# Attention over hop tokens: residual added by VectorE out of PSUM, row variances by ScalarE squares, and a new order inside an iteration

## The chip, the cores and the metric

The kernel runs on one core of a Trainium2 chip. A core has a matrix engine (TensorE; PE in the profile, its weight loads PEld), VectorE (DVE), ScalarE (ACT), GpSimd (POOL) and a queue engine for transfers (SyncE, SP). Each engine works through its own instructions in order; they meet at semaphores. The metric is the device time of one execution in microseconds (us), the median of several runs.

## What is computed

The reference propagates the features of 10,000 nodes seven times over a graph of 160,000 edges, which gives eight tokens of 128 features for each node, and then runs one self-attention block over each node's eight tokens and a weighted readout:

```python
    tok = jnp.stack(toks, axis=1)                      # (N, K+1, D)
    t = _layernorm(tok, axis=-1)
    q   = jnp.einsum('nkd,de->nke', t, wq)
    key = jnp.einsum('nkd,de->nke', t, wk)
    v   = jnp.einsum('nkd,de->nke', t, wv)
    scale = 1.0 / (D ** 0.5)
    attn = _softmax(jnp.einsum('nkd,nld->nkl', q, key) * scale, axis=-1)
    o = jnp.einsum('nkl,nld->nkd', attn, v)
    o = tok + jnp.einsum('nkd,de->nke', o, wo)
    r = _layernorm(o, axis=-1)
    alpha = _softmax(jnp.einsum('nkd,d->nk', r, w_r), axis=-1)
    return jnp.einsum('nk,nkd->nd', alpha, o)
```

All of it is in fp32 in the attention stage.

## The kernel before

First come the hops (class `Hops`, lines 34 to 600), which leave the eight tokens in DRAM as arrays `tok[k]`. The change leaves them as they are. Then `attention` runs. It takes the rows in groups of 16 nodes: 16 nodes x 8 tokens = 128 partitions, 128 features along the free dimension, and 16 groups make a supergroup (`SG`), so there are 40 supergroups, the last one with a single group. Its instructions stand on each engine in the order in which the Python code emits them; nothing reorders them.

The algebra is folded so that the layer norm needs few passes. `M` is the centred product of wq and wk, `Wv` that of wv and wo, with two more columns that give, for each token, a readout term of the value (column 128) and one of the token itself (129). The factor 1/sqrt(variance) of each row is applied later: by rows to the scores, by columns through small products that spread a row's factor over the eight rows of its node (`same_node`, a product with a 0/1 matrix `same`).

For one supergroup i the steps are, with the engine that does them:

- `load` (SP): eight transfers, one for each token index, into the tile `x`; six buffers.
- `xT` (PE, then a copy by ACT): transposes of the 16 groups, four at a time ("quarters", q = 0 to 3).
- `uT` (PE, ACT copy): M times xT, a quarter at a time. `val` (PE, ACT copy): xT times Wv, three groups at a time, into `v`.
- `norms` (DVE): `bn_stats` of the rows of `x` of one supergroup and of the rows of `o` of an older one, then `rstd` for both together: variance, and three Newton steps for the inverse root. It gives `rs` (for the scores) and `lb` (for the readout, from `w`).
- `extras` (DVE): `rb`, the row factor and the value term laid out by token.
- `score` (PE): 64 small products of uT and xT into the PSUM tile `ps`.
- `same_node` (PE): spreads `rb` (of i) and `lb` (of i - 3) into the PSUM tile `sm`.
- `soft1` (DVE), `soft_exp` (ACT), `soft2` (DVE, POOL), `soft3` (DVE transpose, POOL copies): the softmax; the result is a block-diagonal matrix `PT`. `soft2` also gives `w`, the readout logit before its norm.
- `attend` (PE, ACT copy): for each quarter a product of the identity with `x` (the residual) and four products PT times v, summed in one PSUM tile `po`, copied to `o`.
- `read1` (DVE), `read_exp` (ACT), `read2` (DVE, POOL), `read3` (PE), `store` (DVE copy of `f`, SP transfers): the softmax over tokens and the weighted sum.

The loop interleaves the stages of several supergroups. In iteration i it does load(i+3); soft1(i-1); then quarter by quarter xT(i+1), uT(i), val(i), attend(i-2), with norms(i+1, i-3) in two halves, the rest of the softmax of i-1 at quarters 1 and 2, the readout of i-4 at quarters 2 and 3, scores in two halves at quarters 1 and 3, and at the end of quarter 3, in this order on PE, the node sums of i and i-3 and the readout product of i-4; `store(i-4)` closes the iteration. There are 45 iterations, from -1 to 43.

PSUM tiles share buffers by tag: the tiles of xT, uT and val have three between them (tag "a"), `po` has two, `ps`, `sm` and `pf` one each. A PE product into a full set of buffers waits until the reader of the oldest is done.

Of the kernel before, what the change touches and what calls it, by code (L numbers as in the profile page):

```python
# [591 lines left out]
SG = 16  # L592
# [41 lines left out]
def attention(ctx, tc, tok, out, wq, wk, wv, wo, w_r, ngrp=N // 16):  # L634
# [6 lines left out]
    xp, tp, vp, op_, wp, sp = pool("axp", 6), pool("atp", 2), pool("avp", 3), pool("aop", 4), pool("awp", 2), pool("asp", 4)  # L641
    pp = pool("app", 1, space=PSUM)


    ip = cp.tile([128, 128], I32, name="ip")
# [29 lines left out]
    w4 = cp.tile([128, 4, 128], F32, name="w4")  # L675
    for i, w in enumerate((wq, wk, wv, wo)):
        nc.sync.dma_start(w4[:, i, :], w)
# [13 lines left out]
    Wv = cp.tile([128, 130], F32, name="Wv")  # L691
# [18 lines left out]
    def rstd(st):  # L710

        d, v, y, z = (sp.tile([128, 2, SG], F32, name="r" + c) for c in "dvyz")
        V.tensor_tensor(d, st[:, :, :, 1], st[:, :, :, 4], op=ALU.subtract)
        V.scalar_tensor_tensor(d, d, 0.25, d, op0=ALU.mult, op1=ALU.mult)
        V.tensor_tensor(v, st[:, :, :, 2], st[:, :, :, 5], op=ALU.add)
        V.scalar_tensor_tensor(v, v, 1.0 / D, d, op0=ALU.mult, op1=ALU.add)
# [9 lines left out]
    sgs = [(s, min(SG, ngrp - s)) for s in range(0, ngrp, SG)]  # L726
    S = [dict() for _ in sgs]

    def load(i):
        s, n = sgs[i]  # L730
        x = S[i]["x"] = xp.tile([128, SG, 128], F32, name="x")
        for k in range(8):
            src = bass.AP(tensor=tok[k].tensor, offset=tok[k].offset + s * 16 * 128, ap=[[n * 128, 16], [128, n], [1, 128]])
            nc.sync.dma_start(x[k::8, :n, :], src)

    quarters = lambda i, h=None: [(a, min(a + 4, sgs[i][1])) for a in (range(0, SG, 4) if h is None else (8 * h, 8 * h + 4)) if a < sgs[i][1]]
# [23 lines left out]
    def val(i, c):  # L760
        a, b = 3 * c, min(3 * c + 3, sgs[i][1])
        if c == 0:
            S[i]["v"] = vp.tile([128, SG, 130], F32, name="v")
        if a >= b:
            return
        p = pp.tile([128, 512], F32, name="pv", tag="a", bufs=3)[:, :390].rearrange("p (g d) -> p g d", d=130)
# [16 lines left out]
    def score(i, h):  # L783
        if h == 0:
            S[i]["s"] = pp.tile([128, SG, 32], F32, name="ps", tag="s", bufs=1)
        for g in range(8 * h, min(8 * h + 8, sgs[i][1])):
            for c in range(0, 128, 32):
                T.matmul(S[i]["s"][c:c + 32, g, :], S[i]["uT", h][:, g - 8 * h, c:c + 32], S[i]["xT"][:, g, c:c + 32],
                         start=True, stop=True, tile_position=(0, c))
# [15 lines left out]
    def soft1(i):  # L805
        n = sgs[i][1]
        c = wp.tile([128, SG, 4, 8], F32, name="c4")[:, :n]
        V.tensor_tensor(c, S[i]["s"][:, :n].rearrange("p g (n k) -> p g n k", k=8),
                        in4[:, None, :, None].to_broadcast([128, n, 4, 8]), op=ALU.mult)
        rk = wp.tile([128, SG, 8], F32, name="rk")[:, :n]  # L810
        V.tensor_tensor(rk, S[i]["sm"][:, 0, :n], S[i]["rs"][:, :, None].to_broadcast([128, n, 8]), op=ALU.mult)
        e = S[i]["e"] = wp.tile([128, SG, 8], F32, name="e")[:, :n]
        V.tensor_reduce(e, c.rearrange("p g n k -> p g k n"), axis=X, op=ALU.add)
        V.tensor_mul(e, e, rk)
# [4 lines left out]
    def soft_exp(i):  # L819
        A.activation(S[i]["e"], S[i]["e"], AF.Exp)  # L820

    def soft2(i):
# [11 lines left out]
        y = wp.tile([128, SG, 8], F32, name="y")[:, :n]  # L834
        V.tensor_tensor(y, e, S[i]["sm"][:, 1, :n], op=ALU.mult)
# [12 lines left out]
    def norms(i, j, h):  # L848
        if h == 0:
            st = norms.st = sp.tile([128, 2, SG, 6], F32, name="st")  # L850
            if not (ok(i) and ok(j)) or sgs[i][1] < SG:
                V.memset(st, 1.0)
        st = norms.st
        if ok(i):
            for g in range(8 * h, min(8 * h + 8, sgs[i][1])):
                V.bn_stats(st[:, 0, g, :], S[i]["x"][:, g, :])  # L856
        if ok(j):
            for g in range(8 * h, min(8 * h + 8, sgs[j][1])):
                V.bn_stats(st[:, 1, g, :], S[j]["o"][:, g, :])  # L859
        if h == 1:  # L860
            y = rstd(st)
            if ok(i):
                S[i]["rs"] = y[:, 0, :sgs[i][1]]
            if ok(j):
                n = sgs[j][1]
                l = S[j]["l"] = sp.tile([128, SG], F32, name="l")[:, :n]
                V.tensor_mul(l, S[j]["w"], y[:, 1, :n])
                r = S[j]["lb"] = wp.tile([128, SG, 8], F32, name="lb")
                V.tensor_tensor(r[:, :n], l[:, :, None].to_broadcast([128, n, 8]), id8[:, None, :].to_broadcast([128, n, 8]), op=ALU.mult)
# [36 lines left out]
    def store(i):  # L906
        s, n = sgs[i]
        f = wp.tile([128, 2, 128], F32, name="f")
        for h in range(0, n, 8):
            m = min(8, n - h)  # L910
            V.tensor_copy(f[:16 * m, h // 8, :], S[i]["f"][:16 * m, h // 8, :])
# [6 lines left out]
    load(0)  # L918
    load(1)
    for i in range(-1, n + 4):  # L920
        if ok(i + 3):
            load(i + 3)
        if ok(i - 1):
            soft1(i - 1)
        for q in range(4):
            if q == 1 and ok(i - 1):
                soft_exp(i - 1)
                soft2(i - 1)
            if q == 2 and ok(i - 4):
                read1(i - 4)  # L930
            if q == 2 and ok(i - 1):
                soft3(i - 1)
            if q == 3 and ok(i - 4):
                read_exp(i - 4)
                read2(i - 4)
            if q % 2 == 0:
                norms(i + 1, i - 3, q // 2)
            if ok(i + 1):
                xT(i + 1, q)
            if ok(i):  # L940
                uT(i, q)
                for c in ((0,), (1, 2), (3, 4), (5,))[q]:
                    val(i, c)
            if ok(i - 2):
                attend(i - 2, q)
            if q % 2 == 1 and ok(i):
                if q == 3:
                    extras(i)
                score(i, q // 2)
            if q == 3:  # L950
                sm = pp.tile([128, 4, SG * 8], F32, name="sm", tag="m", bufs=1).rearrange("p a (g k) -> p a g k", k=8)
                if ok(i):
                    S[i]["sm"] = sm
                    m = sgs[i][1]
                    same_node(sm[:, 0:2, :m], S[i]["rb"][:, :, :m])
                if ok(i - 3):
                    m = sgs[i - 3][1]
                    S[i - 3]["lc"] = sm[:, 2, :m]
                    same_node(sm[:, 2, :m], S[i - 3]["lb"][:, :m])
                if ok(i - 4):  # L960
                    read3(i - 4)
        if ok(i - 4):
            store(i - 4)


# [37 lines left out]
```

## Time and profile before

| What | us | Where from |
|---|---|---|
| Median of three runs | 4508.32 | times (4507.62 to 4515.4) |
| The profiled execution | 4508.36 | its own time |
| Its span | 4506.6 | page |
| PE busy in the span | 4015.8 (89%) | page, part 1 |
| DVE busy | 3529.0 (78%) | page, part 1 |
| ACT busy | 2521.5 (56%) | page, part 1 |
| POOL busy | 1256.0 (28%) | page, part 1 |
| First instruction of the attention stage (SP, weights) | 3670.58 | order of time of SP |
| One steady iteration | 19.90 to 19.93 | eight periods from 3872.60 on |
| PE, DVE, ACT, POOL busy in it | 19.18, 17.03, 9.84, 4.35 | mean of the eight periods |

Matmuls are pipelined and their ends are modelled, so a busy PE is not PE at its peak. A line of the order of time gives the start of a run of like instructions, how long the run lasted, engine, source line, operation, output and input tiles with their shapes, how many, and in brackets how long the engine was idle before it and who released it. DVE and ACT start the next instruction a little before the last one's recorded end; the distance from start to start is what an instruction costs its engine. An fp32 product shows as two records.

### The profile page before, as it was taken

The numbers are of one execution on the slowest core, as the hardware profiler recorded it, in microseconds if no ns is written. First come the engines' busy times: TensorE is split into PE (matmuls) and PEld (weight loads), VectorE is DVE, ScalarE is ACT, GpSimd is POOL, SyncE is SP. The second block draws the span as 40 slices with busy tenths as digits, with TensorE's granted clock in tenths as the row PEclk, the third lists the DMA queues.
The fourth block names the chain that finished last, engine by engine and source line by source line (L and its number), as shares of the span: only waits on it lengthen the run. The fifth ranks groups of instructions, "written<-read, shape, count | busy, mean of one in ns | idle before, by whom it ended". The sixth has DMA issues, their size and how long they took to land.

```text
span 4506.6 us, 170913 instructions
## 1 busy us (share of the span) xinstructions
PE 4015.8 (89%) x74352; PEld 3266.3 (72%) x74352; DVE 3529.0 (78%) x7740; ACT 2521.5 (56%) x5159; POOL 1256.0 (28%) x1423
## 2 busy tenths in 40 slices
PE   0566389999998999999999999999999989999996
PEld 0456366766766888888888888888888867777774
DVE  5888799999996777777777777777766668888887
ACT  3000036565666777777777777777766645544542
POOL 0000024334343333333333333333333322222221
PEclk9887689999998999999999999999999989999998
DMA  3000044454455555555555555555555541221210
GB/s 115 1 1 1 1 132 149 140 155 149 142 154 187 182 180 177 183 185 183 178 182 181 179 182 184 177 184 184 181 163 169 164 128 52 65 63 56 65 56 10
DMA packets 296789, 588.20 MB, mean 131 GB/s; under 512 B 46895, under 2 KB 198541, under 8 KB 290781
## 3 DMA queue, kind: packets, MB, share of 16 engines
q1 hardware_dynamic: 218893, 509.90, 34.3%
q0 software_dynamic: 17696, 36.28, 3.8%
q10 hardware_dynamic: 59440, 31.03, 2.4%
q8 instruction: 582, 9.54, 0.8%
q14 instruction: 178, 1.46, 0.1%
HBM read 447.66 MB, written 129.38 MB: 128 GB/s over the span
## 4 chain that ended last, share of the span: by engine, by line
PE 51%; DVE 32%; issue 9%; DMA 4%; POOL 2%; ACT 1%; SPq 1%; ACTq 0%; DVEq 0%; POOLq 0%
PE p L442 20%; PE acc L426 20%; PE ta L270 3%; DVE w L406 3%; DVE st L859 3%; DVE st L856 2%; DVE o L183 2%; DVE w L403 2%; DMA rb<-srow 2%; DVE ro L265 2%; PE tb L335 1%; POOL r L461 1%; DVE R L183 1%; DVE oh L177 1%; DVE ux L190 1%
## 5 line engine op out<-in xcount | busy, mean ns | idle before, releaser
L445 ACT CAST eb<-p 128x512 f16<-128x512 f32 x3634 | 1859.9, 607 | 738.9 <-PE p L442 723.6
L445 DVE CAST eb<-p 128x512 f16<-128x512 f32 x1896 | 1180.2, 683 | 461.3 <-PE p L442 460.7
L442 PE MATMUL p<-tab,w 128*32 128x256 f16 x44240 | 1426.2, 274 | 30.1 <-ACT eb L445 14.3
L426 PE MATMUL acc<-eb,w 128*128 128x256 f16 (+1 forms) x11060 | 1409.4, 274 | 3.1 <-DVE indeg L483 3.0
L442 PEld LDWEIGHTS <-w 128*32 128x32 fp8e4 x44240 | 1118.1, 96 | 268.2 <-issue 185.4
L418 POOL DMA_INDIRECT og<-tabd,oidx x553 | 620.4, 1122 | 2217.8 <-PE acc L432 1426.1
L426 PEld LDWEIGHTS <-w 128*128 128x128 fp8e4 x11060 | 1019.2, 98 | 270.5 <-issue 156.4
L461 POOL TENSOR_SCALAR r<-s,ctok 128x128 f32<-128x128 f32 x553 | 451.2, 816 | 341.4 <-DVE indeg L483 170.5
L560 DVE SCALAR_TENSOR_TENSOR tab<-s,c,tab 128x128 f16<-128x128 f32 x395 | 139.2, 352 | 182.5 <-ACT tab L559 181.1
L434 DVE TENSOR_REDUCE s<-acc 128x128 f32<-128x256 f32 x553 | 234.2, 423 | 41.2 <-PE acc L432 30.7
L406 DVE TENSOR_TENSOR w<-dsl,iof 128x2560 fp8e4<-128x2560 f16 x79 | 222.5, 2816 | 1.2 <-ACT dsl L351 1.2
L257 ACT ACTIVATE U<-U 128x160 f16<-128x160 f32 x25 | 7.6, 304 | 384.5 <-PE U L250 384.5
L768 PEld LDWEIGHTS pv<-Wv,xT 128*128 128x128 f32 x1250 | 165.1, 192 | 75.7 <-issue 57.0
L780 PEld LDWEIGHTS po<-v,pT 128*128 128x128 f32 x1250 | 164.4, 192 | 74.8 <-issue 74.8
L270 PE MATMUL ta<-o,ro 128*128 128x160 f16 x1250 | 132.0, 284 | 93.3 <-DVE ro L265 93.3
L781 ACT COPY o<-po 128x512 f32<-128x512 f32 (+1 forms) x157 | 91.8, 584 | 210.9 <-PE po L780 210.9
L270 PEld LDWEIGHTS <-ro 128*128 128x128 f16 x1250 | 127.0, 121 | 97.4 <-DVE ro L265 97.0
L559 ACT ACTIVATE tab<-s,c 128x128 f16<-128x128 f32 x395 | 158.6, 401 | 62.0 <-DVE s L434 7.4
L748 ACT COPY xT<-pt 128x512 f32<-128x512 f32 (+1 forms) x157 | 91.1, 580 | 166.0 <-PE pt L747 165.9
L768 PE MATMUL pv<-Wv,xT 128*128 128x130 f32 x1250 | 165.8, 276 | 0.0
L780 PE MATMUL po<-v,pT 128*128 128x128 f32 x1250 | 165.1, 275 | 0.0
L250 PE MATMUL U<-oh,tri 128*128 128x80 f16 x1250 | 62.2, 221 | 114.7 <-DVE oh L177 114.7
(245 smaller groups left out, 4291.4 us busy)
## 6 DMA issues: line engine op xcount, KB each, us to landing
w<-gsd SPq DMA_DIRECT2D x474, 640.0 KB
rb<-srow SPq DMA_DIRECT2D x79, 640.0 KB
gsd<-w SPq DMA_DIRECT2D x79, 640.0 KB
tok<-r SPq DMA_DIRECT2D x546, 64.0 KB
x<-tok SPq DMA_DIRECT2D x273, 128.0 KB
tabd<-tab ACTq DMA_DIRECT2D x395, 64.0 KB
og<-tabd,oidx POOLq DMA_INDIRECT x553, 4.0
x<-in_x SPq DMA_DIRECT2D x39, 128.0 KB
```

Of the source, the lines that this page charges most:

```text
L270: T.matmul(ta, ro[:, j, :, i], o12[:, j, :, i], start=j + i == 0, stop=j + i == NP)
L406: V.tensor_tensor(w[:, NJ * 128:].rearrange("p (j d) -> p j d", d=128), dsl[:, g, :, None].to_broadcast([128, NJ, 128]), self.iof1[:, None ...
L418: G.indirect_dma_start(out=og, out_offset=None, in_=tabd, in_offset=bass.IndirectOffsetOnAxis(ap=self.oidx[:, t:t + 1], axis=0))
L426: T.matmul(acc[:, :m], w[:, (NJ + J) * 128:(NJ + J + 1) * 128], e[:, j, :m], start=J == 0, stop=False)
L434: V.tensor_reduce(s, acc[:, 0:256].rearrange("p (h d) -> p d h", h=2), axis=X, op=ALU.add)
L442: T.matmul(p[32 * q:32 * q + 32, j], w[:, s * CAP:(s + 1) * CAP], tab[:, s, :], start=True, stop=True)
L445: (A.copy if evac(jj) else V.tensor_copy)(e[:, :, 0:256], p.rearrange("p j h d -> p j (h d)"))
L461: self.nc.gpsimd.tensor_scalar(r, s, ct[:, t:t + 1], None, op0=ALU.mult)
L559: A.activation(new[:, t, 0:128], s, AF.Copy, scale=c1[:, t:t + 1])
L560: V.scalar_tensor_tensor(new[:, t, 128:256], s, c1[:, t:t + 1], new[:, t, 0:128], op0=ALU.mult, op1=ALU.subtract)
L768: T.matmul(p[:, g - a, :], S[i]["xT"][:, g, :], Wv, start=True, stop=True)
L780: T.matmul(p[:, g - a, :], PT[i % 2][:, g, :], S[i]["v"][:, g, :128], start=False, stop=g == b - 1, skip_group_check=True)
```

## The change

The parts of the diff, in the order of one iteration:

- `attend` no longer multiplies the identity with `x` and no longer has ACT copy the result. A new `resid` has VectorE add `po` (PSUM) and `x` (SBUF) into `o`.
- The rows of `x` no longer go through `bn_stats`. A new `squares` has ScalarE compute (x0 - x)^2 for each group, x0 being the row's first feature, with the sum along the row as a second output (`sq`); a new column 130 of `Wv` gives, out of `val`, the row's mean of x relative to x0 up to sign, and `norms` takes its square from the mean of squares.
- `bn_stats` of `o` stand apart in `stats`; `norms(i, i-3)` runs once an iteration, at quarter 2, and calls `extras` itself.
- In `soft1a` a reduce over four becomes two adds. The readout term in column 129 is copied by ACT into a ninth column of `y` and summed by the reduce that was there already; before, an add did it.
- ACT copies `f` in `store`; before, VectorE did.
- Within an iteration `val` comes in quarters 0 and 1, `uT` in 2 and 3, and all scores at the end. The node sums `sm` of i-1 and i-4 and the readout product of i-5 follow the first quarter's transposes, an iteration later than before; there are 46 iterations, from -1 to 44.
- Supergroup 0 is loaded through ACT's queue, and the weights and this load come ahead of the set-up of constants.

```diff
+    load(0, nc.scalar)
...
-    Wv = cp.tile([128, 130], F32, name="Wv")
+    Wv = cp.tile([128, 131], F32, name="Wv")
...
+    V.tensor_scalar(Wv[:, 130:131], ident[:, 0:1], -1.0, 1.0 / D, op0=ALU.mult, op1=ALU.add)
...
-        T.matmul(p[:, :b - a], ident, S[i]["x"][:, a:b, :], start=True, stop=False, skip_group_check=True)
         for g in range(a, b):
-            T.matmul(p[:, g - a, :], PT[i % 2][:, g, :], S[i]["v"][:, g, :128], start=False, stop=g == b - 1, skip_group_check=True)
-        A.copy(S[i]["o"][:, a:b, :], p[:, :b - a])
+            T.matmul(p[:, g - a, :], PT[i % 2][:, g, :], S[i]["v"][:, g, :128], start=True, stop=True)
+        S[i]["po", q] = p
+
+    def resid(i, q):
+        a, b = 4 * q, min(4 * q + 4, sgs[i][1])
+        if a < b:
+            V.tensor_tensor(S[i]["o"][:, a:b, :], S[i]["po", q][:, :b - a], S[i]["x"][:, a:b, :], op=ALU.add)
+
+    def squares(i, q):
+
+        if q == 0:
+            S[i]["sq"] = sp.tile([128, SG], F32, name="sq")
+        for g in range(4 * q, min(4 * q + 4, sgs[i][1])):
+            j = jp.tile([128, 128], F32, name="junk")
+            A.activation(j, S[i]["x"][:, g, :], AF.Square, bias=S[i]["x"][:, g, 0:1], scale=-1.0, accum_out=S[i]["sq"][:, g:g + 1])
...
+        d = wp.tile([128, SG, 2, 8], F32, name="c2")[:, :n]
+        V.tensor_tensor(d, c[:, :, 0:2], c[:, :, 2:4], op=ALU.add)
+        e = S[i]["e"] = wp.tile([128, SG, 8], F32, name="e")[:, :n]
+        V.tensor_tensor(e, d[:, :, 0], d[:, :, 1], op=ALU.add)
...
-        V.tensor_reduce(e, c.rearrange("p g n k -> p g k n"), axis=X, op=ALU.add)
...
     def soft_exp(i):
+        n = sgs[i][1]
+        y = S[i]["y"] = wp.tile([128, SG, 9], F32, name="y")[:, :n]
+        A.copy(y[:, :, 8:9], S[i]["v"][:, :n, 129:130])
         A.activation(S[i]["e"], S[i]["e"], AF.Exp)
...
-        V.tensor_tensor(w, w, S[i]["v"][:, :n, 129], op=ALU.add)
...
+            V.tensor_mul(d, S[i]["v"][:, :n, 130], S[i]["v"][:, :n, 130])
+            V.scalar_tensor_tensor(v[:, 0, :n], S[i]["sq"][:, :n], 1.0 / D, d, op0=ALU.mult, op1=ALU.subtract)
...
-            V.tensor_copy(f[:16 * m, h // 8, :], S[i]["f"][:16 * m, h // 8, :])
+            A.copy(f[:16 * m, h // 8, :], S[i]["f"][:16 * m, h // 8, :])
```

The body of the loop after the change:

```python
    for i in range(-1, n + 5):

        if ok(i + 3):
            load(i + 3)
        if ok(i - 1):
            soft1a(i - 1)
        for q in range(4):
            if ok(i + 1):
                xT(i + 1, q)
            if q == 0:
                sm = pp.tile([128, 4, SG * 8], F32, name="sm", tag="m", bufs=1).rearrange("p a (g k) -> p a g k", k=8)
                if ok(i - 1):
                    S[i - 1]["sm"] = sm
                    m = sgs[i - 1][1]
                    same_node(sm[:, 0:2, :m], S[i - 1]["rb"][:, :, :m])
                    soft1b(i - 1)
                if ok(i - 4):
                    m = sgs[i - 4][1]
                    S[i - 4]["lc"] = sm[:, 2, :m]
                    same_node(sm[:, 2, :m], S[i - 4]["lb"][:, :m])
                if ok(i - 5):
                    read3(i - 5)
            if ok(i):
                for c in range(3 * q, 3 * q + 3) if q < 2 else ():
                    val(i, c)
                for c in range(2 * q - 4, 2 * q - 2) if q >= 2 else ():
                    uT(i, c)
            if q == 0 and ok(i - 1):
                soft_exp(i - 1)
            if q == 1 and ok(i - 4):
                read_exp(i - 4)
            if ok(i + q // 2):
                squares(i + q // 2, (q + 2) % 4)
            if q == 0 and ok(i - 5):
                store(i - 5)
            if ok(i - 2):
                attend(i - 2, q)
            if q == 3 and ok(i):
                score(i)

            if q < 2 and ok(i - 3):
                stats(i - 3, 8 * q, 8 * q + 8)
            if q == 2 and ok(i - 4):
                read2(i - 4)
            if q == 2:
                norms(i, i - 3)
            if ok(i - 2):
                resid(i - 2, q)
            if q == 0 and ok(i - 1):
                soft2(i - 1)
                soft2b(i - 1)
            if q == 0 and ok(i - 4):
                read1(i - 4)
            if q == 1 and ok(i - 1):
                soft3(i - 1)
```

More of the change, by code (lines that the diff above doesn't have):

```diff
@@ L640, in attention, with load @@
     cp = pool("acp", 1)
-    xp, tp, vp, op_, wp, sp = pool("axp", 6), pool("atp", 2), pool("avp", 3), pool("aop", 4), pool("awp", 2), pool("asp", 4)
+    xp, tp, vp, op_, wp, sp, jp = (pool(*a) for a in (("axp", 6), ("atp", 2), ("avp", 3), ("aop", 4), ("awp", 2), ("asp", 4), ("ajp", 2)))
     pp = pool("app", 1, space=PSUM)
+    sgs = [(s, min(SG, ngrp - s)) for s in range(0, ngrp, SG)]
+    S = [dict() for _ in sgs]
+    def load(i, queue=nc.sync):
+        s, n = sgs[i]
+        x = S[i]["x"] = xp.tile([128, SG, 128], F32, name="x")
+        for k in range(8):
+            src = bass.AP(tensor=tok[k].tensor, offset=tok[k].offset + s * 16 * 128, ap=[[n * 128, 16], [128, n], [1, 128]])
+            queue.dma_start(x[k::8, :n, :], src)
+    w4 = cp.tile([128, 4, 128], F32, name="w4")
+    for i, w in enumerate((wq, wk, wv, wo)):
+        nc.sync.dma_start(w4[:, i, :], w)
+    load(0, nc.scalar)
     ip = cp.tile([128, 128], I32, name="ip")
@@ L708, in attention, with rstd @@
         AB.append(a)
[L710 to L716, printed above, removed]
+    def rstd(v):
+        y, z = (sp.tile([128, 2, SG], F32, name="r" + c) for c in "yz")
         V.tensor_scalar(v, v, 1e-5, None, op0=ALU.add)
@@ L724, in rstd @@
         return y
[L726 to L736, printed above, removed]
     def xT(i, q):
@@ L845, in soft3, with stats @@
             G.tensor_copy(PT[i % 2][c:c + 32, :n, c:c + 32], t[c:c + 32, :n * 32].rearrange("p (g k) -> p g k", k=32))
[L848 to L853, printed above, removed]
+    def stats(j, a, b):
+        if a == 0:
+            S[j]["st"] = sp.tile([128, SG, 6], F32, name="st")
+        for g in range(a, min(b, sgs[j][1])):
+            V.bn_stats(S[j]["st"][:, g, :], S[j]["o"][:, g, :])
@@ L854, in norms @@
+    def norms(i, j):
+        v = sp.tile([128, 2, SG], F32, name="rv")
+        if not (ok(i) and ok(j)) or sgs[i][1] < SG:
+            V.memset(v, 1.0)
         if ok(i):
-            for g in range(8 * h, min(8 * h + 8, sgs[i][1])):
-                V.bn_stats(st[:, 0, g, :], S[i]["x"][:, g, :])
+            n = sgs[i][1]
+            d = sp.tile([128, SG], F32, name="rx")[:, :n]
+            V.tensor_mul(d, S[i]["v"][:, :n, 130], S[i]["v"][:, :n, 130])
+            V.scalar_tensor_tensor(v[:, 0, :n], S[i]["sq"][:, :n], 1.0 / D, d, op0=ALU.mult, op1=ALU.subtract)
@@ L857, in norms @@
         if ok(j):
[L858 to L869, printed above, removed]
+            n = sgs[j][1]
@@ new lines, in norms @@
+            st = S[j]["st"][:, :n]
+            d = sp.tile([128, SG], F32, name="rd")[:, :n]
+            V.tensor_tensor(d, st[:, :, 1], st[:, :, 4], op=ALU.subtract)
+            V.scalar_tensor_tensor(d, d, 0.25, d, op0=ALU.mult, op1=ALU.mult)
+            V.tensor_tensor(v[:, 1, :n], st[:, :, 2], st[:, :, 5], op=ALU.add)
+            V.scalar_tensor_tensor(v[:, 1, :n], v[:, 1, :n], 1.0 / D, d, op0=ALU.mult, op1=ALU.add)
+        y = rstd(v)
+        if ok(j):
+            n = sgs[j][1]
+            l = S[j]["l"] = sp.tile([128, SG], F32, name="l")[:, :n]
+            V.tensor_mul(l, S[j]["w"], y[:, 1, :n])
+            r = S[j]["lb"] = wp.tile([128, SG, 8], F32, name="lb")
+            V.tensor_tensor(r[:, :n], l[:, :, None].to_broadcast([128, n, 8]), id8[:, None, :].to_broadcast([128, n, 8]), op=ALU.mult)
@@ L872, in read1 @@
+        if ok(i):
+            S[i]["rs"] = y[:, 0, :sgs[i][1]]
+            extras(i)
     def read1(i):
@@ L944, in attention @@
+            if q == 0 and ok(i - 5):
+                store(i - 5)
             if ok(i - 2):
                 attend(i - 2, q)
[L946 to L961, printed above, removed]
@@ L966, in nagphormer_kernel @@
+            if q == 1 and ok(i - 1):
+                soft3(i - 1)
 @with_exitstack
```

58 lines of the change are left out of this document (25 added, 33 removed).

## The prediction, made before the changed kernel ran

> **What bounds the kernel now.** I first read busy shares and chain on the page, then cut the end of the span into the loop's periods and read every engine's order of time in one of them. Before 3670 us the program is the seven hops, which the change leaves alone; the attention stage is the last 836 us. In its steady part an iteration starts every 19.92 us. One period by engine (columns: PE, PEld, DVE, ACT, POOL busy, clock, DMA share, GB/s):
>
> ```profile
> 3892.52:3912.45 19.93, 19.17 (x275) 14.58 (x274) 17.04 (x74) 9.84 (x20) 4.35 (x7) 1.00 0.20 61
> ```
>
> PE and DVE are both nearly full, ACT half empty; the clock is full. The order of time of DVE in it (start, duration):
>
> ```profile
> 3892.52 1.65 DVE L856 BATCH_NORM_STATS2 st<-x 128x6 f32<-128x128 f32 x8
> 3894.08 1.63 DVE L859 BATCH_NORM_STATS2 st<-o 128x6 f32<-128x128 f32 x8
> 3895.63 0.27 DVE L826 TENSOR_REDUCE z<-e 128x16 f32<-128x128 f32 x1
> ...
> 3906.99 0.29 DVE L801 TENSOR_TENSOR rb<-v,id 128x128 f32<-128x128 f32 x1
> 3909.13 0.49 DVE L911 COPY f<-pf 128x128 f32<-128x128 f32 x2 [1.85 <-PE pf L903]
> 3909.54 0.68 DVE L808 TENSOR_TENSOR c<-ps,in 128x512 f32<-128x512 f32 x1
> 3910.14 0.28 DVE L811 TENSOR_TENSOR rk<-sm,ry 128x128 f32<-128x128 f32 x1
> 3910.34 1.07 DVE L813 TENSOR_REDUCE e<-c 128x128 f32<-128x512 f32 x1
> 3911.44 0.29 DVE L814 TENSOR_TENSOR e<-e,rk 128x128 f32<-128x128 f32 x1
> ```
>
> DVE runs without a gap from 3892.52 to 3907.28, waits 1.85 for PE, and runs on to 3912.46: 18.09 of work and one wait. In that wait PE does what DVE's last tile released, the node sums and the readout:
>
> ```profile
> 3907.33 0.64 PE L794 MATMUL sm<-rb,same 128*32 128x256 f32 x8 [0.76 <-DVE rb L801]
> 3907.79 0.40 PE L794 MATMUL sm<-lb,same 128*32 128x128 f32 x8
> 3908.01 1.05 PE L903 MATMUL pf<-o,Ab 128*32 128x128 f32 x32
> ```
>
> So the period is a ring through DVE (18.09) and the PE pieces at its end (1.85). PE alone, by starts of its groups (xT 4 x 0.44, uT 4 x 0.86, identity 4 x 0.86, val 16 x 0.218, attend 16 x 0.216, score 2 x 0.70, sums 0.68, readout 1.0), is 18.7: it would bind next.
>
> **The change, part by part; per iteration of 16 groups.**
>
> *Residual.* PE loses four 128x512 fp32 products with the identity, each two records 0.43 apart (3895.47 to 3896.33): -3.44, leaving 15.3. ACT loses its four `o` copies (0.59 busy, 0.49 from start to next). DVE gains four adds of a 128x512 PSUM tile. The nearest row is L808, same shape and also out of PSUM: 0.60 to the next start; upper end 0.68, that row's whole duration. I take 0.60: +2.40.
>
> *Statistics of x.* DVE loses 16 bn_stats: 1.56 + 1.52 = -3.08. Two small operations come in (`rx`, its combination with `sq`), dependent, 0.25 + 0.20 as L713 and L714 stand; four others are half as wide: together +0.35. The extra column of Wv widens val's products by 1 of 130: nothing. ACT gets 16 squares of 128x128 with a per-partition bias and a summed output. The trace has no such sum. Lower end, a row of the same size with a per-partition operand and no sum:
>
> ```profile
> L161 ACT ACTIVATE tab<-tab,disT 128x128 f32<-128x128 f32 x79 | 23.2, 387 | 0.0
> ```
>
> 23.2/79 = 0.294 from one to the next. Upper end: 0.387 without overlap and a read-out as dear as the smallest ACT row (Exp of 128x8, 0.212): 0.60. I take c = 0.39, no overlap and a cheap read-out, nearer the row that it resembles most.
>
> *Scores' sum.* The reduce (1.10) becomes two adds. 128x256 lies between 0.32 (128x128 dependent, L814) and 0.72 (128x512 dependent); I take 0.45, the other 0.32, and 0.12 because the next operation now hangs on `c`: -0.21.
>
> *Moved off DVE.* The `f` copies (-0.41) go to ACT (2 x 0.18 start to next); the add `w+v` (-0.41) becomes a column copied by ACT (0.11) and one more column in a reduce (+0.02).
>
> *The wait of 1.85.* The node sums and the readout now follow an iteration's first transposes, and what they need (rb, lb, Ab) left DVE and POOL in the iteration before; the `f` copy is ACT's. DVE has nothing at that place any more. -1.85.
>
> Sum on DVE: 18.09 - 3.08 - 0.21 - 0.41 - 0.41 + 2.40 + 0.35 + 0.02 = **16.75**, if it never waits.
>
> **Does it wait?** Before the first add DVE does 2.7 (scores) and 1.55 (eight stats): 4.3 after its start. PE's first attend ends 0.44 + 0.46 + 0.22 + 1.0 + 1.96 + 0.86 + 0.25 (last matmul to reader) = 5.2 after the iteration's first transpose. PE must lead by 0.9. It can: its work is 1.45 shorter, and what holds it back, the sums' wait for `rb`, lets go two adds (1.2) before DVE's iteration ends, with 0.44 of transposes ahead of it: a lead of 1.6. Cover gone, it costs about 0.7.
>
> ACT now carries waits with a queue behind them. Its exp waits for DVE's `e`, 2.7 after DVE's start, with four squares, two `f` copies and the next xT and v copies behind it, and PE wants those buffers at the sixth val product. With the lead of 1.6, `e` is there at 4.3 of PE's time; ACT ends its third v copy at 4.7. No wait, but PE then waits some 0.9 for that xT copy, out of its 1.45.
>
> The ring of PE and ACT is the second bound: ACT's pieces from the first v copy to the last uT copy, 7.1 without squares, twelve squares, then the second half of the scores 0.70, transposes 0.44, sums 0.68, readout 1.0, val 0.65 and 0.25 to reader, under which four squares hide: 10.9 + 12c. At c = 0.39 it is 15.5, at 0.60 18.1; it passes 16.75 at c = 0.49. Either bound, whichever is larger: **P = 16.75**; ends 16.5 (the half-size add at 0.32, the narrower operations hidden) and 18.1.
>
> *SP and POOL.* The stores stand behind eight loads in SP's queue, as before; the loads wait for `x` of three iterations back, last read at that iteration's end now as then, and are needed two iterations later. POOL's 4.35 are unchanged; PT is done some 13 us into an iteration and wanted in the next.
>
> *Start.* Group 0 is loaded from ACT's queue, beside the weights on SP's:
>
> ```profile
> 3672.88 0.64 SPq L734 DMA_DIRECT2D x<-in_x  x1
> 3673.56 4.37 SPq L734 DMA_DIRECT2D x<-tok  x7
> 3677.97 0.59 SPq L734 DMA_DIRECT2D x<-in_x  x1
> ```
>
> Group 1's issues move from 3677.97 to about 3672.9; PE now waits for that group at 3686.34 (1.83, DMA x<-in_x) after 3.03 for group 0. About -4.8. ACT's eight issues end near 3676, before its first copy at 3682. Iteration 1 loses its 2.48 wait for `rb`, iterations 2 and 3 the identity, 3.4 each: together -14; I book -12, as the same load shares the DMA engines (181 GB/s there).
>
> *End.* Iterations 38 to 43 took 75.7. One more is run. DVE's sums for the seven, from the same rows: 16.8, 16.9, 13.4, 8.7, 5.6, 4.8, 3.8 = 70, with two of them only the empty rstd, and some 4 of waits on the way readout takes: -2. It may be +6 if that way waits more.
>
> **Sum.** 34 periods (iterations 4 to 37) x (19.92 - 16.75) = 107.8; 107.8 + 12 + 2 = 122. The profiled execution took 4508.36 (span 4506.6), the median of the runs 4508.32, so no correction: **4387 us**.
>
> **Rivals.**
> - *ACT becomes the bound* (c 0.5 to 0.75). For it: a sum has to be read out of the engine, and no row shows that. Against: the spare 10 us of ACT. c = 0.60: P = 18.1, 34 x 1.82 + 14 = 76, 4432 us.
> - *DVE waits for the first attend*, if PE gets no lead: +0.7 to 0.9, P = 17.55, 4414 us. Against: PE's 1.45 spare.
> - *Slower: the summed square costs double.* If reading the sum drains ACT so that a square takes c = 0.79 or more (two unoverlapped passes of 0.39), 10.9 + 12c = 20.4 exceeds the old period by what start and end give: the point of decision. At c = 0.9, P = 21.7: 4508 + 34 x 1.78 - 14 = 4555 us.
> - *Slower by function tables*: square and exp alternate four times an iteration; if they sat in different tables, four loads at the one load's 1.28 us (L161) add 5.1 to the ring: 15.5 + 5.1 = 20.6, 4517 us. Against: the built order of the changed kernel has one load, in the hops, as before. [...]
> - *It doesn't do what it says*: the freed time turns into waits among PE, ACT and DVE, and the period stays at 19.9: 4494 to 4508.
>
> **How the numbers follow.** Forecast 0.60, ACT-bound 0.20, first-attend wait 0.09, nothing gained 0.04, double-cost squares 0.06, tables 0.01. Low end: P = 16.5, all 14 of the start, and 12 at the end, where DVE now waits 2.6 for the readout in each of the last four iterations: 4508 - 116 - 26 = 4366. High end: c = 0.60, 4432. That leaves out the slower cases, no gain, and the worse part of ACT-bound, under 0.2. A measurement of this kernel can tell about 0.2% (9 us) from no change: faster 0.89, same 0.04, slower 0.07.
>
> **What would show it.** Right: a period near 16.75 with DVE gapless, the adds 0.60 apart, PE near 15.3 with short waits for ACT's copies and `rb`, squares near 0.39. Wrong: squares over 0.49 apart and DVE waiting for `ps` or `po` (the ring binds); DVE waiting at the first add alone (no lead); table loads in the stage; a tail over 80 us.

## The result, and the profile after

The changed kernel is slower: 4567.1 us median of four runs (4560.23 to 4569.08) against 4511.13 (4507.62 to 4515.4) for the kernel before, a ratio of 1.0121 (95% interval 1.0103 to 1.0138). The forecast was 4387, and its range ended at 4432.

The profiled execution took 4560.23 us, 51.9 more than that of before. The hops take the same time in both traces within 0.7 us (the first weight transfer behind them is at 3670.58 before and at 3671.20 after); the difference lies in the attention stage. Between the `c` (scores times column factors, DVE's first work on the scores) of iterations 4 and 39, 35 periods apart, there are 748.8 us instead of 695.3: +53.5. Up to the first of these `c` 2.45 were gained, and behind the last one the tail cost 0.8. So the question is why an iteration takes 21.39 us on average (mostly 21.13, 21.13 or 20.9, and 22.4 in turn) where 16.75 was forecast and 19.91 was the time before.

The engines' busy time over 600 us of the steady part of the changed kernel (window, length, then PE, PEld, DVE, ACT and POOL busy, the granted clock as a share of TensorE's full clock, DMA share, GB/s):

```profile
3800.00:4400.00 600.00, 505.87 (x7378) 408.75 (x7376) 458.96 (x1726) 375.79 (x1418) 118.68 (x196) 0.89 0.20 57
```

No engine is full any more: DVE is busy for 76%, PE for 84%, and PE's granted clock, 1.00 in this stretch before, averages 0.89. An engine that binds on its own would be full, so this is waiting. The waits of the same stretch say who waits for whom (total, times, longest):

```profile
DVE o L781 <- PE po L775: 111.3, 28, 5.0
...
PE sm L801 <- DVE rk L826: 60.0, 28, 2.1
...
PE sm L801 <- DVE rb L808: 13.0, 28, 0.5
```

In each of 28 iterations DVE waits once for PE, at the first residual add, 111.3/28 = 3.98 us; and PE waits once for DVE, 2.14 us, in front of the second product into `sm`. DVE's work without waits is about 17.45 (shown below), and 17.45 + 3.98 = 21.4 is the period. The order of time of PE shows what lies between the two waits:

```profile
4000.15 0.63 PE L743 MATMUL pt<-ident,x 128*128 128x128 f32 x4 [0.26 <-PE ps L795]
4001.18 0.64 PE L801 MATMUL sm<-rb,same 128*32 128x256 f32 x8 [0.40 <-DVE rb L808]
4003.96 0.65 PE L801 MATMUL sm<-lb,same 128*32 128x128 f32 x8 [2.14 <-DVE rk L826]
4004.39 1.93 PE L932 MATMUL pf<-o,Ab 128*32 128x128 f32 x32
4006.25 2.82 PE L764 MATMUL pv<-Wv,xT 128*128 128x131 f32 x18
4008.91 1.05 PE L775 MATMUL po<-v,pT 128*128 128x128 f32 x8
...
4025.06 0.65 PE L801 MATMUL sm<-lb,same 128*32 128x128 f32 x8 [2.14 <-DVE rk L826]
...
4027.35 4.19 PE L764 MATMUL pv<-Wv,xT 128*128 128x131 f32 x18
```

And the same time on DVE, with the first add of the next iteration as the last line:

```profile
4000.43 0.29 DVE L895 TENSOR_TENSOR lb<-l,id 128x128 f32<-128x128 f32 x1
...
4002.24 0.68 DVE L815 TENSOR_TENSOR c<-ps,in 128x512 f32<-128x512 f32 x1
...
4003.63 0.28 DVE L826 TENSOR_TENSOR rk<-sm,ry 128x128 f32<-128x128 f32 x1
...
4004.80 1.64 DVE L870 BATCH_NORM_STATS2 st<-o 128x6 f32<-128x128 f32 x8
4010.01 0.69 DVE L781 TENSOR_TENSOR o<-po,x 128x512 f32<-128x512 f32 x1 [3.57 <-PE po L775]
...
4032.47 0.69 DVE L781 TENSOR_TENSOR o<-po,x 128x512 f32<-128x512 f32 x1 [4.94 <-PE po L775]
```

Three things are to be seen. First, `lb`, which the second product needs, is there from 4000.72 on, 3.2 us before 4003.96; PE waits until DVE has read `rk` out of the part of `sm` that the first product wrote. In the loop, `soft1b(i - 1)`, which reads it, is emitted between the two `same_node` calls, and both write one PSUM tile. DVE comes to `rk` only after two adds and the whole of `soft1a`. Second, after that idle time the same products run longer: the readout product 1.93 instead of 1.05 before, nine `val` products 2.82 or 4.19. Third, the first attend is late by all this, and DVE, which has the stats to do and then nothing, stands still for 3.57 or 4.94. PE waits for DVE and then DVE for PE: they take turns.

The granted clock of the changed kernel, one microsecond at a time around the first of these gaps (columns as above):

```profile
4002.00:4003.00 1.00, 0.00 (x0) 0.00 (x0) 0.96 (x3) 0.00 (x0) 0.00 (x0) 1.00 0.00 0
4003.00:4004.00 1.00, 0.04 (x4) 0.04 (x6) 0.93 (x4) 0.00 (x0) 0.00 (x0) 0.99 0.06 25
4004.00:4005.00 1.00, 1.00 (x20) 0.92 (x24) 0.93 (x4) 0.00 (x0) 0.00 (x0) 0.50 0.80 270
...
4007.00:4008.00 1.00, 1.00 (x9) 1.00 (x8) 0.00 (x0) 0.23 (x1) 0.00 (x0) 0.80 0.69 262
...
4024.00:4025.00 1.00, 0.00 (x0) 0.00 (x0) 0.93 (x4) 0.00 (x0) 0.00 (x0) 0.73 0.43 115
...
4031.00:4032.00 1.00, 1.00 (x9) 1.00 (x9) 0.00 (x0) 0.42 (x2) 0.00 (x0) 0.85 0.00 0
```

It is halved from 3.98 to 7.40 past 4000 (the means of 0.99 and 0.80 in the first and last of these microseconds say where), and around the next gap, by the last two lines and 0.50 between them, from 4024.46 to 4031.30.

Some of the forecast's own terms can be read here too. From the page of the changed kernel, groups of instructions (busy, mean ns of one | idle time before them):

```profile
L789 ACT ACTIVATE junk<-x 128x128 f32<-128x128 f32 x625 | 243.2, 399 | 0.0
...
L781 DVE TENSOR_TENSOR o<-po,x 128x512 f32<-128x512 f32 (+1 forms) x157 | 103.5, 680 | 141.8 <-PE po L775 141.8
```

An add takes 0.68 and 0.60 to the next start, as costed; 141.8 us over the whole stage go on waiting for the first of four. And two squares on ACT, in order of time:

```profile
4009.83 0.39 ACT L789 ACTIVATE junk<-x 128x128 f32<-128x128 f32 x1
4010.12 0.19 ACT L789 ACTIVATION_READ_ACCUMULATOR junk<-x 128x1 f32 x1
4010.21 0.39 ACT L789 ACTIVATE junk<-x 128x128 f32<-128x128 f32 x1
```

The sum comes out through an instruction of its own, 0.19 long; from square to square it is 0.38, where 0.39 was taken.

### The profile page after: what moved, and what is told of

It is laid out like the page before. It is cut to its first block, busy times and chain, and to the rows that moved or that the text cites. A ratio compares the mean times of both kernels' runs of the same rounds, so it can differ in the third digit from the quotient of the medians.

```text
span 4558.4 us, 171149 instructions
## 1 busy us (share of the span) xinstructions
PE 3966.3 (87%) x74038; PEld 3261.4 (72%) x74038; DVE 3502.9 (77%) x7266; ACT 2664.7 (58%) x6371; POOL 1255.5 (28%) x1423
## 4 chain that ended last, share of the span: by engine, by line
PE 55%; DVE 30%; issue 8%; DMA 3%; ACT 2%; POOL 2%; ACTq 0%; SPq 0%; POOLq 0%; DVEq 0%
PE p L442 21%; PE acc L426 21%; PE ta L270 3%; DVE w L406 3%; PE pv L764 3%; DVE o L183 2%; DVE o L781 2%; DVE w L403 2%; PE tb L335 1%; DVE ro L265 1%; PE pf L932 1%; DMA rb<-srow 1%; DVE st L870 1%; DVE R L183 1%; DVE oh L177 1%
## 5 line engine op out<-in xcount | busy, mean ns | idle before, releaser
L765 ACT COPY v<-pv 128x393 f32<-128x393 f32 x235 | 98.3, 460 | 262.6 <-PE pv L764 262.6
L789 ACT ACTIVATE junk<-x 128x128 f32<-128x128 f32 x625 | 243.2, 399 | 0.0
L764 PE MATMUL pv<-Wv,xT 128*128 128x131 f32 x1250 | 205.7, 323 | 23.3 <-ACT xT L744 23.3
L764 PEld LDWEIGHTS pv<-Wv,xT 128*128 128x128 f32 x1250 | 186.7, 231 | 45.9 <-ACT xT L744 31.0
L781 DVE TENSOR_TENSOR o<-po,x 128x512 f32<-128x512 f32 (+1 forms) x157 | 103.5, 680 | 141.8 <-PE po L775 141.8
L847 POOL TENSOR_TENSOR p<-e,in 128x512 f32<-128x512 f32 (+1 forms) x40 | 40.8, 1019 | 560.8 <-DVE e L845 560.8
```

The source lines that it names most:

```text
L781: V.tensor_tensor(S[i]["o"][:, a:b, :], S[i]["po", q][:, :b - a], S[i]["x"][:, a:b, :], op=ALU.add)
L789: A.activation(j, S[i]["x"][:, g, :], AF.Square, bias=S[i]["x"][:, g, 0:1], scale=-1.0, accum_out=S[i]["sq"][:, g:g + 1])
```

## The experiments

All times stand beside runs of the kernel before on the same chip: 4519.83 (4516.89 to 4524.89, seven runs) for e1 to e4, 4520.03 (4515.49 to 4524.97, seven runs) for e5, e6, e7 and e9, and 4509.93 (one run) for e8.

The theory: the wait for `rk` holds PE, PE's idle time halves its clock, and both together are the loss. The rivals: the wait is for a value, or for something else that comes at the same time; the clock does it all, or nothing; the freed work was never on the path.

### e1: both node sums ahead of `soft1b`

```diff
                     same_node(sm[:, 0:2, :m], S[i - 1]["rb"][:, :, :m])
-                    soft1b(i - 1)
                 if ok(i - 4):
                     ...
                     same_node(sm[:, 2, :m], S[i - 4]["lb"][:, :m])
+                if ok(i - 1):
+                    soft1b(i - 1)
                 if ok(i - 5):
                     read3(i - 5)
```

> Edit: soft1b is emitted after both node sums instead of between them. Theory (shared tile and clock): the second node sums wait for VectorE's rk only because rk reads another part of the same PSUM tile sm; that idle 2.1 us also halves TensorE's clock for the 4 to 7 us behind it. Without it: no wait at the second sums, clock near 1.00, VectorE without gaps, a period of 17.4 to 17.8 (VectorE's own 17.5) for the changed kernel's 21.4, 4560 - 35 x 3.9 = about 4425 us. Rival (the ring between TensorE and VectorE is there anyway, since TensorE gets no lead): only the wait of 2.1 goes, period 19.3, about 4487 us.

Measured: 4437.83 us (4430.9 to 4439.12, four runs), a ratio of 0.9815 (0.9798 to 0.9831) to before. No instruction is added or taken away; `soft1b` and the second sums change places. The period is 17.45, and the clock is 1.00 over 500 us of the steady part. The order of time of PE in e1, and then a line of DVE:

```profile
4009.44 0.64 PE L801 MATMUL sm<-rb,same 128*32 128x256 f32 x8 [0.77 <-DVE rb L808]
4009.89 0.40 PE L801 MATMUL sm<-lb,same 128*32 128x128 f32 x8
4010.11 1.06 PE L932 MATMUL pf<-o,Ab 128*32 128x128 f32 x32
...
4013.21 1.05 PE L775 MATMUL po<-v,pT 128*128 128x128 f32 x8
```

```profile
4014.62 0.67 DVE L781 TENSOR_TENSOR o<-po,x 128x512 f32<-128x512 f32 x1
```

The wait for `rk` is gone, the readout product is back at 1.06, and DVE runs through its first add (4014.62) without a gap: the attend's last product ends at 4014.26, 0.36 earlier. What the changed kernel lost is here: 35 x (21.39 - 17.45) is about 138 us.

### e2: the order as changed, `lc` in another tile

```diff
-                    S[i - 4]["lc"] = sm[:, 2, :m]
-                    same_node(sm[:, 2, :m], S[i - 4]["lb"][:, :m])
+                    S[i - 4]["lc"] = pf[:, 2, :].rearrange("p (g k) -> p g k", k=8)[:, :m]
+                    same_node(pf[:, 2, :].rearrange("p (g k) -> p g k", k=8)[:, :m], S[i - 4]["lb"][:, :m])
```

The tile of the readout product gets a third part and is made ahead of the sums.

> Edit: the order stays as changed, but the readout's sums lc lie in the tile of pf, another PSUM bank than sm. Theory (it is the shared tile that makes the second sums wait, no value of rk): as in the run with the sums together, period within 0.3 of it, about 4425 us. Rival (the sums wait for VectorE because of their place in the order or for lb): the wait of 2.1 at the second sums stays and the period stays 21.4, about 4560 us.

Measured: 4437.69 us (one run), period 17.45. With the emission order of the changed kernel, the loss is gone as well: in its trace the second product starts 0.46 behind the first (4008.07 and 4008.53), without a wait. So no value was waited for: the second product and `rk` touch different columns, and what ordered them is that they share a tile. In e2 `lc` lies in another tile and so at another place in PSUM; which of the two counts, no run tells apart.

### e3 and e8: work for PE in the gap

```diff
                     soft1b(i - 1)
+                    if ok(i - 4):
+                        fill = pp.tile([128, 512], F32, name="fill", tag="a", bufs=3)
+                        for _ in range(2):
+                            T.matmul(fill, ident, w4.rearrange("p a d -> p (a d)"), start=True, stop=True)
```

In e8 the loop runs once. The product is read by nobody; it stands in the changed kernel's order, in the 2.14 us where PE waits.

> Edit: the changed kernel as it is, with four records of TensorE work whose result nobody reads (0.43 each) put into the gap ahead of the second sums. Theory (the idle time brings the clock down): the clock stays 1.00, the readout product takes 1.0 instead of 1.93 and the first nine value products 2.0 instead of 2.8 to 4.2, the period falls to about 19.4 although TensorE has more to do, 4560 - 35 x 2.0 = 4490 us. Rival (the records are slow for another reason, for instance the transfers that run at the same time): they stay slow and the period stays at 21.4 or over, 4560 us or more.

> Edit: the changed kernel with two records of unread TensorE work (0.86 us in all) ahead of the second sums, half of the earlier fill. Theory (the idle time brings the clock down once it is long enough; 0.5 to 0.8 us at a time did not, 0.4 + 2.1 did): 1.3 us of idle are left; if that is short enough, the clock stays at 1.00 and the period is 19.5 as with the whole fill, about 4509 us; if not, 21.4 and 4560 to 4575 us. Rival (the fill helped by something else than the clock, in proportion to its length): a period between, near 20.4.

Measured: e3 4508.97 us, e8 4493.39 us (one run each); periods 19.51 and 19.52. The clock is 1.00 over 500 us of the steady part of e3; e8 has the same mean over its whole run (0.958, against 0.944 in the changed kernel's profiled run), and the products behind its gap are as long as in e3 (readout 1.06, nine `val` products 2.28). PE in e3, then in e8:

```profile
4013.81 0.64 PE L801 MATMUL sm<-rb,same 128*32 128x256 f32 x8 [0.48 <-DVE rb L808]
4014.38 1.98 PE L967 MATMUL fill<-w,ident 128*128 128x512 f32 x4
4016.59 0.43 PE L801 MATMUL sm<-lb,same 128*32 128x128 f32 x8 [0.23 <-DVE rk L826]
4016.84 1.06 PE L932 MATMUL pf<-o,Ab 128*32 128x128 f32 x32
4017.82 2.28 PE L764 MATMUL pv<-Wv,xT 128*128 128x131 f32 x18
```

```profile
4002.37 0.43 PE L801 MATMUL sm<-lb,same 128*32 128x128 f32 x8 [1.09 <-DVE rk L826]
```

PE does 1.98 us more work in an iteration, and the iteration is 1.88 shorter. The wait for `rk` still stands in it, filled; the clock does not fall. That divides the loss: 21.39 - 19.51 = 1.9 by the clock, 19.51 - 17.45 = 2.06 by the wait itself; DVE's wait at its first add is 1.96 in e3 (51.0 us in 26 waits over 500 us). Half the filling (idle 0.49 and 1.09) does the same as the whole.

### e4: POOL's copies of `PT` away from DVE's short operations

In e1, gapless, DVE's work is 17.45, not the 16.75 of the forecast. Two operations in `norms` stand out, at the time when POOL copies `PT`. In e1, on DVE and then on POOL:

```profile
4004.36 0.52 DVE L886 SCALAR_TENSOR_TENSOR rd<-rd 128x16 f32<-128x16 f32 x1
...
4005.01 0.52 DVE L888 SCALAR_TENSOR_TENSOR rv<-rv,rd 128x16 f32<-128x16 f32 x1
```

```profile
4002.95 2.56 POOL L863 COPY pT<-t 32x512 f32<-32x512 f32 x4 [3.04 <-DVE t L861]
```

POOL's four copies take 0.64 each from start to start, so the third ends at about 4004.87 and the fourth at 4005.51. The two operations on DVE end at 4004.88 and 4005.53, each with a copy.

e4 is e1 with `soft3` (DVE's transpose, then these copies) behind `norms`:

```diff
             if q == 2:
                 norms(i, i - 3)
+            if q == 2 and ok(i - 1):
+                soft3(i - 1)
...
-            if q == 1 and ok(i - 1):
-                soft3(i - 1)
```

> Edit: sums together as in the first run, and soft3 (VectorE's transpose, GpSimd's copies into PT) is emitted after norms. Theory (GpSimd's copies stretch VectorE's small two-input operations in norms, 0.43 to 0.53 instead of 0.19, 1.1 us in all): those rows are back at 0.19, period 16.4 to 16.7, 1.1 less than with the sums together alone, about 4388 us. Rival (they are long for what they read, not for GpSimd): rows as long as before, no gain. Second rival (PT comes too late): TensorE waits for GpSimd's copies at the first attend and the gain is lost.

Measured: 4414.58 us (4412.26 to 4415.31, four runs), ratio 0.9766 (0.975 to 0.9783); period 16.84. The same operations on DVE in e4:

```profile
4008.90 0.27 DVE L886 SCALAR_TENSOR_TENSOR rd<-rd 128x16 f32<-128x16 f32 x1
...
4009.31 0.17 DVE L888 SCALAR_TENSOR_TENSOR rv<-rv,rd 128x16 f32<-128x16 f32 x1
```

They take 0.27 and 0.17 instead of 0.52 each. The gain is 0.61 an iteration where 1.1 had been expected. Some of the stretching moved with the copies: `e<-c` (L820), 0.29 in e1, takes 0.58 in 37 of the 40 iterations of e4. In the last of them (a supergroup with a single group) POOL's four copies run from 4369.69 to 4372.24, 0.64 each; L820 takes 0.53 and ends at 4371.60, L827 takes 0.54 and ends at 4372.25, beside the ends of the third and the fourth copy. From start to start L820 and the add before it (L818) take 0.51 and 0.53 in e4, 0.21 and 0.46 in e1, so some 0.37 of stretching is left. What the two engines share there, no run shows.

### e5: the trims together

e4 with two edits at the ends: group 0 loaded on SP's queue again, and no empty `norms` in the last iterations.

```diff
-    load(0, nc.scalar)
+    load(0)
...
-            if q == 2:
+            if q == 2 and (ok(i) or ok(i - 3)):
                 norms(i, i - 3)
```

> Edit on top of the kernel with PT later: group 0 loaded through SP's queue again, ahead of group 1, and norms skipped where neither of its supergroups exists. Theory (groups 0 and 1 loaded side by side share the transfer engines, so group 0 comes later, 12.3 us after the first weight transfer instead of 10.3; and the last two norms run on VectorE after the output is on its way): group 0's transposes start some 10.3 after the first weight transfer, the end comes about 3 earlier, period unchanged at 16.84: about 4409 us. Rival (start and end are set by other work): within 1 us of 4414.

Measured: 4407.72 us (4403.58 to 4409.25, four runs), ratio 0.9752 (0.9736 to 0.9768): the fastest of all kernels here. From the first weight transfer to the first transpose of group 0 it takes 9.35 us, against 12.86 in e4 (and 10.28 before, 12.25 after the change): the load on ACT's queue was a loss. From the last `c` (the supergroup with a single group) to the end it is 39.1 instead of 41.85.

### e6: the residual alone, in the old order

The kernel before, with the identity product and ACT's copy replaced by the add on DVE.

```diff
-        T.matmul(p[:, :b - a], ident, S[i]["x"][:, a:b, :], start=True, stop=False, skip_group_check=True)
         ...
-        A.copy(S[i]["o"][:, a:b, :], p[:, :b - a])
+        V.tensor_tensor(S[i]["o"][:, a:b, :], p[:, :b - a], S[i]["x"][:, a:b, :], op=ALU.add)
```

> Edit: the kernel before with only the residual moved (no product with the identity, no copy by ScalarE; VectorE adds x to po). Theory (before, VectorE and the node sums form the ring, so work taken from TensorE gains nothing and VectorE's four adds cost 2.4): period 22.3, more if TensorE's longer idle time brings its clock down, up to 24.5: 4594 to 4670 us. Rival (TensorE was the bound): period falls by up to 3.4, below 4500 us.

Measured: 4668.6 us (one run), period 23.9 to 24.0, the clock 0.85 over 400 us of the steady part. The node sums in it, at the old place at the end of an iteration:

```profile
4000.52 1.08 PE L793 MATMUL sm<-rb,same 128*32 128x256 f32 x8 [6.07 <-DVE rb L800]
...
4001.80 1.93 PE L902 MATMUL pf<-o,Ab 128*32 128x128 f32 x32
```

DVE's 18.09 + 2.40 = 20.5 of work, and its wait for the readout, 1.85 before, is now 3.34: behind PE's idle 6.07 these products run at half clock (1.08 and 1.93 for 0.64 and 1.05). 20.5 + 3.34 = 23.8. In the kernel before, the add alone costs 4 us an iteration.

### e7: the statistics of `x` back on DVE

e1 with `bn_stats` of `x` in place of ACT's squares.

```diff
-            j = jp.tile([128, 128], F32, name="junk")
-            A.activation(j, S[i]["x"][:, g, :], AF.Square, bias=S[i]["x"][:, g, 0:1], scale=-1.0, accum_out=S[i]["sq"][:, g:g + 1])
+            V.bn_stats(S[i]["sx"][:, g, :], S[i]["x"][:, g, :])
```

> Edit: the kernel with the sums together, but the rows of x go through bn_stats on VectorE again, not through ScalarE's squares. Theory (with the sums together VectorE alone is the bound): its 17.45 grow by 16 x 0.194 less 0.35 of smaller operations to about 20.2, about 4533 us on the chip where the sums together took 4438. Rival (ScalarE's queue is the bound): the period falls.

Measured: 4535.64 us (one run), period 20.43: the squares are worth 20.43 - 17.45 = 3.0 an iteration.

### e9: the identity product back on PE

e1 with the residual as before.

```diff
+        T.matmul(p[:, :b - a], ident, S[i]["x"][:, a:b, :], start=True, stop=False, skip_group_check=True)
         ...
+        A.copy(S[i]["o"][:, a:b, :], p[:, :b - a])
...
-            V.tensor_tensor(S[i]["o"][:, a:b, :], S[i]["po", q][:, :b - a], S[i]["x"][:, a:b, :], op=ALU.add)
```

> Edit: the kernel with the sums together, but the residual is done by the product with the identity and ScalarE's copy again. Theory: VectorE falls to 15.05 and TensorE's work rises from 15.3 to 18.7, with its short waits for ScalarE a period of 19.0 to 19.8, about 4505 us. Rival (TensorE has room): a period below 17.45.

Measured: 4520.45 us (one run), periods mostly 19.75 to 21.0, about 20.0, a little over the 19.8 at which the expectation ended. PE is busy for 389.2 of 400 us, and DVE waits for it at the scores. The wait in e9:

```profile
DVE c L816 <- PE ps L796: 68.1, 20, 3.5
```

So with the sums together the residual on DVE is worth some 2.5 an iteration: it takes the identity product, costed at 3.44, off PE, which binds in e9, and with the adds on it DVE is the next bound, at 17.45.

## Why the prediction was wrong

**The step that failed** is "*The wait of 1.85*", and its repetition under "Does it wait?". The text says that "DVE has nothing at that place any more" and that "what holds it back, the sums' wait for `rb`", lets go early enough for PE to lead by 1.6. The wait for `rb` is there and small (0.46 on average, 0.5 at most). What the step left out is a second thing that holds PE, one product later: the second `same_node` shares its tile with the first, and DVE's read of the first stands between them. That could be read off the loop. DVE's 1.85 of waiting became PE's 2.14, and came back to DVE as 3.98. e1 and e2 take it away in two ways and give the same time within 0.2 us.

**A cost that no term held** is the clock. The trace of before has it at 1.00 in the steady part, where PE idles once in an iteration, for 0.75 on average and 1.1 at most, so its rows give no price for a longer gap. e3 gives it: 1.9 of the 3.94 between the periods of the changed kernel and of e1.

**The rival nearest to it** was "DVE waits for the first attend", with the right place and 0.09 of the chance, but priced at 0.7 to 0.9: only a lead that is not there, with no wait for `rk` and no idle time put into PE. The sign named for it ("DVE waiting at the first add alone") is what the waits show. The rivals on the slower side, double-cost squares and tables, did not happen: 0.38 from square to square, and no table load in the stage (the program's one load, 1.28 at 23.30, is in the hops). Nor was ACT the bound: in e4, with the same squares, the period is 16.84.

**DVE's sum** was 16.75. It is 17.45 where it can be seen without waits (e1), and 16.84 once POOL's copies stand elsewhere (e4). The 0.6 is the neighbour that the short operations got in the new order. That 16.84 lies so near to 16.75 is in part luck: without the 0.37 of stretching that e4's rows still hold, the same work would take some 16.5 (an estimate), so the additions and removals came out nearly 0.3 smaller than forecast. The prediction said that POOL's work is "unchanged"; the work is, its place against DVE's is not.

**The squares** were put at -3.08 and +0.35, thus -2.73 with the operations that replace them; e7 has 3.0. **PE's work** was to fall by 3.44; it fell by 3.2, to 15.95 busy in a period of e1 (457.16 in 500 us) from 19.18. **The lead** that PE needs is there with the sums together, but thin: 0.36 to spare where 1.6 - 0.9 = 0.7 was worked out.

**Start and end** were to give 12 and 2. They gave 2.45 and -0.8. The load through ACT's queue, booked as a gain of 4.8, was a loss of 2.0 to 3.5: before, SP issues group 0's seven transfers in 4.37. In the changed kernel, with two queues at it, ACT's order of time has group 0 and SP's has group 1:

```profile
3670.56 8.75 ACTq L652 DMA_DIRECT2D x<-tok  x7
```

```profile
3674.59 6.98 SPq L652 DMA_DIRECT2D x<-tok  x7
```

Both take longer, and the first transposes wait for the whole of group 0. DVE's empty `norms` at the end show in e5's tail, 2.75 shorter.

With the two lines changed over (e1), the ratio 0.9815 would make 4428 of the 4511 of this chip: inside the range, at its slow end. So the parts, added up, were close, in part by luck; their order on PE was not followed product by product.

What stays open: e2, e3, e6, e7, e8 and e9 have one run each, so their times are good to some 10 us; what they show rests on their periods. Which of e5's two edits gave how much of the 7 us is known only from the two distances in its trace. The 0.37 of DVE's stretching by POOL that is left in e4 is read from its rows alone; no run takes it away.

## What to carry to other kernels

When a step is moved ahead on one engine, list for each of its instructions every earlier reader of the tile that it writes, other columns included, and where that reader stands in its own queue: a reader emitted between two writers of one PSUM tile ordered all three of them here. An idle time put into TensorE can cost more than its own length: here 2.1 us of waiting brought another 1.9 by the clock, so a gap of this size on PE (2.54 with the shorter one before it) is priced with the products behind it at half speed, if another engine waits for those. A trade between engines (the residual) can be a loss of 4 us an iteration in one kernel (e6, where DVE still has the statistics of `x` and PE waits for it) and a gain of 2.5 in another (e1 against e9, where PE binds and DVE has room); it is to be judged in the kernel in which it will stand. How much of that turn comes from the order and how much from the squares no run tells apart.

## What the runs showed of the hardware

In these runs 2.54 us of idle time were enough to bring the clock down, and it did not fall after the same idle time each time. In the changed kernel 0.40 and 2.14 of idle time with 0.64 of work between them brought it from 1.00 to 0.50; behind 0.49 and 1.09 in e8 the readout product took 1.06, as at 1.00. In e7 PE has one gap an iteration, of 2.65 to 2.98 in most of them and of about 4.5 in every ninth. The readout product behind it, in two iterations of e7 with gaps of the same length:

```profile
3982.23 0.64 PE L800 MATMUL sm<-rb,same 128*32 128x256 f32 x8 [2.96 <-DVE rb L807]
...
3982.90 1.30 PE L934 MATMUL pf<-o,Ab 128*32 128x128 f32 x32
```

```profile
4002.66 0.64 PE L800 MATMUL sm<-rb,same 128*32 128x256 f32 x8 [2.97 <-DVE rb L807]
...
4003.34 1.06 PE L934 MATMUL pf<-o,Ab 128*32 128x128 f32 x32
```

The second gap leaves the clock alone (1.00 in each microsecond from 4001 to 4008), the first does not, and the drop comes only after work has resumed (in an earlier iteration PE resumes at 3859.65, and the clock is 1.00 from 3859 to 3860 and 0.84 in the microsecond after it). In the six iterations from 3880 on, the readout product takes 1.55, 1.50, 1.45, 1.40, 1.35 and 1.30. Its part behind the drop runs at half speed, so that each 0.05 less means a drop 0.05 later. An estimate that fits this: idle time counts over fixed stretches of time, which these iterations beat against. The clock records in the changed kernel's trace give their length: from 3800 to 4400 there are 28 times at half clock, each 3.41 or 6.83 long and each beginning 20.48 or 23.89 after the one before, which is one, two, six and seven stretches of 3.413; and six of them are 0.05 more than e7's period of 20.43.

From this follows an estimate of the idle time that it takes in e7. At 1.30 the drop lies 2 x 1.06 - 1.30 = 0.82 behind the start of the readout product, at 3983.72, and 1.92 of the gap (3980.31 to 3982.23) lie in the stretch of 3.41 before it. Six stretches later, at 4004.20, it is 1.87 of the other gap (4000.79 to 4002.66), and the clock stays. So, by this estimate, about 1.9 us of idle time in one stretch make the difference there; the changed kernel has 2.54 in the stretch that ends at 3.98 past 4000, in two gaps, and e8 no more than 1.58. Counted in the same way from 3800 to 4400 of the changed kernel (waits of 0.16 and more), each of the 28 stretches at full clock with 1.92 or more of idle time is followed by half clock, none of those with 0.66 or less is, and no stretch lies between.

In e7 the low clock (0.91 on average over 400 us) costs little, since DVE binds there (busy for 379.35 of these 400 us) and waits for PE at its adds for 0.7 in all: its iterations are 20.43 or, with the clock low longest, 20.9.
